# Regrouping a decode backward kernel: four groups of two kv-heads over all batches, and the zero rows as 6 KB packets on one queue

## Chip, cores and metric

One core of a Trainium2 chip. The metric is the device time of one execution in microseconds (us); "span" is the time from the first to the last instruction of the profiled execution, some 1 to 5 us shorter. Engines: PE (TensorE), DVE (VectorE), ACT (ScalarE), POOL (GpSimd), SP (SyncE, used here only to start transfers).

## The reference

A decode step of one token for four batches: attention over the last 1024 of 4096 cached positions (32 query heads, 8 kv-heads of 128), and a GEGLU feed-forward part (512 to 1792), both added to x. What is computed is the output and all gradients.

```python
def _A_ref(x, k_cache, v_cache, wq, wo):
    ...
    W = min(4096, max(256, Sk // 4))                      # 1024 of 4096
    q = (lambda x, *d: x.transpose(*d))((x @ wq).reshape(B, Sq, Hq, Dh), 0, 2, 1, 3)
    k = jnp.repeat(k_cache[:, :, Sk - W:, :], rep, axis=1)
    v = jnp.repeat(v_cache[:, :, Sk - W:, :], rep, axis=1)
    scores = jnp.einsum("bhqd,bhkd->bhqk", q, k) * (Dh ** -0.5)
    p = _softmax(scores, axis=-1)
    o = jnp.einsum("bhqk,bhkd->bhqd", p, v)
    ...
x = A_x
xn = _layernorm(x, axis=-1)
return x + _A_ref(xn, A_k_cache, A_v_cache, A_wq, A_wo) + _B_ref(xn, B_w_gate, B_w_up, B_w_down)
# outputs: that, and jax.vjp of it: dx, dK, dV, dwq, dwo, dw_gate, dw_up, dw_down
```

The gradients of the caches have the caches' size, and three quarters of them are zeros: 50.3 MB of the 81.0 MB that are written.

## The kernel before

Weights first, then the feed-forward part, then one batch after another. Each piece of zeros waits for a point in the scores; each transposed block is copied half by ACT, half by DVE.

```python
        def emit_zero_pieces(step, gate_ap):
            target = (len(zero_pieces) * (step + 1) + nsteps - 1) // nsteps
            while zdone[0] < min(target, len(zero_pieces)):
                nc.gpsimd.affine_select(out=ztile[:], in_=gate_ap, pattern=[[0, ZW]], compare_op=ALU.is_ge,
                                        fill=0.0, base=-1, channel_multiplier=0)
                nc.gpsimd.dma_start(out=zero_pieces[zdone[0]], in_=zsrc)      # 2 MB, rows of 2,048 B
                zdone[0] += 1
        for b in range(B):
            ...
            for g in range(G):
                ...
                    nc.scalar.copy(out=T_sb[:, 0:hw], in_=T_ps_flat[:, 0:hw])
                    nc.vector.tensor_copy(out=T_sb[:, hw:J * P], in_=T_ps_flat[:, hw:J * P])
                ...
            for lhs_src, rmask, og, tg in ((P_b, domr, out_3, "dv"), (dS_b, qmr, out_2, "dk")):
                ...
                        nc.tensor.matmul(mps[:], lhsT=lhs_src[:, j * P:(j + 1) * P], rhs=rhs, start=True,
                                         stop=True)                             # all 128 rows
                ...
                    nc.sync.dma_start(out=dst_full, in_=stg[:].rearrange("p g j d -> p g (j d)"))
    # then: gradients of wo and wq, and wo and wq read once more for the output and dx
```

## Time and profile before

| | before |
|---|---|
| time, median of 3 (range) | 389.94 us (388.05 to 392.74) |
| span, mean granted PE clock | 385.1 us, 0.785 |
| moved by DMA | 120.48 MB, 313 GB/s over the span |

The lines that matter are in the prediction. They show a kernel that changes between stages that are full of transfers and stages in which DMA stands half idle.

### The profile page before, as it was taken

To read this page: it belongs to the slowest core of one execution; us is meant where nothing else is said; L and a number is where in the kernel's file an instruction comes from. 1 tells how busy PE (TensorE), PEld (TensorE's weight loads), DVE (VectorE), ACT (ScalarE), POOL (GpSimd) and SP (SyncE) were. 2 spreads that over 40 slices of the span, in tenths; PEclk is the share of its full clock that TensorE was granted. 3 is DMA by queue.
4 is the path that set the end of the run, shared out by engine and by line. 5 is a ranking of instruction groups with operands and counts; after the bars stand their busy time and mean duration, and the time that the engine had idled before them with its cause. 6 is when DMAs were issued, how large, how long until landed. Compare 5 with 4: busy or idle time off the path is not lost.

```text
span 385.1 us, 6390 instructions
## 1 busy us (share of the span) xinstructions
PE 276.8 (72%) x2524; PEld 143.0 (37%) x2524; DVE 180.3 (47%) x344; ACT 156.2 (41%) x257; POOL 72.7 (19%) x103
## 2 busy tenths in 40 slices
PE   0087897998367949994999489968809768874882
PEld 0075553446133624462546253635206221110340
DVE  3034242545973366636573658355904233331425
ACT  1045253553233535654575437552705332430431
POOL 1000132535565222102202110222222211100000
PEclk9999595896657966997699959995966655555997
DMA  7999999358676649997999699956996999996350
GB/s 269 394 397 418 401 393 366 149 206 323 257 283 265 267 145 397 413 409 283 366 410 410 270 350 376 409 231 265 414 360 247 356 400 403 401 319 218 111 163 1
DMA packets 55181, 120.48 MB, mean 313 GB/s; under 512 B 3360, under 2 KB 21552, under 8 KB 54640
## 3 DMA queue, kind: packets, MB, share of 16 engines
q1 hardware_dynamic: 40400, 64.25, 45.6%
q0 software_dynamic: 14752, 55.84, 36.0%
q8 instruction: 19, 0.31, 0.3%
q14 instruction: 10, 0.08, 0.1%
HBM read 39.07 MB, written 81.01 MB: 312 GB/s over the span
## 4 chain that ended last, share of the span: by engine, by line
PE 32%; DMA 25%; DVE 13%; ACT 13%; issue 9%; SPq 5%; POOL 4%; DVEq 0%; ACTq 0%; POOLq 0%
DMA out_dram<-osb 10%; PE kv_ps L466 9%; ACT T_sb L400 8%; DMA vb<-in_A_v_cache_dram 6%; PE S_ps L404 4%; SPq L159 4%; PE dP_ps L404 3%; DMA wo_sb<-in_A_wo_dram 3%; DMA out_dram<-stg_dk 3%; PE dxa_ps L559 2%; DVE osb L87 2%; DMA wq_c<-in_A_wq_dram 2%; DVE stg_dk L87 2%; POOL out_dram L307 2%; PE od_ps L451 2%
## 5 line engine op out<-in xcount | busy, mean ns | idle before, releaser
L377 POOL TENSOR_SCALAR_AFFINE_SELECT ztile<-vb 128x1024 bf16<-128x1024 bf16 x24 | 25.0, 1043 | 224.5 <-DMA out_dram<-ztile 185.4
L400 ACT COPY T_sb<-T_ps 128x512 bf16<-128x512 bf16 x64 | 37.1, 586 | 38.2 <-PE T_ps L94 35.2
L401 DVE COPY T_sb<-T_ps 128x512 bf16<-128x512 bf16 x64 | 26.9, 422 | 39.0 <-ACT T_sb L400 38.8
L94 PE MATMUL T_ps<-ident,vb 128*128 128x128 bf16 x256 | 28.4, 227 | 0.9 <-DVE T_sb L401 0.9
L404 PE MATMUL dP_ps<-T_sb,dom 128*128 128x512 bf16 x64 | 24.3, 393 | 6.5 <-DVE negm L412 4.0
L94 PE MATMUL T_ps<-ident,kb 128*128 128x128 bf16 x256 | 28.9, 230 | 0.0
L404 PE MATMUL S_ps<-T_sb,qm 128*128 128x512 bf16 x64 | 24.3, 394 | 4.2 <-DVE osb L87 2.3
L466 PE MATMUL kv_ps<-domr,P_b 128*128 128x512 bf16 x64 | 26.9, 533 | 0.5 <-DVE stg_dv L87 0.2
L85 ACT CAST stg_dv<-kv_ps 128x512 bf16<-128x512 f32 x32 | 18.7, 585 | 17.8 <-PE kv_ps L466 17.2
L87 DVE CAST stg_dv<-kv_ps 128x512 bf16<-128x512 f32 x32 | 21.8, 691 | 7.3 <-PE kv_ps L466 6.7
L94 PEld LDWEIGHTS <-kb 128*128 128x128 bf16 x256 | 20.2, 104 | 11.8 <-issue 6.2
L94 PEld LDWEIGHTS <-vb 128*128 128x128 bf16 x256 | 19.8, 102 | 11.8 <-issue 6.0
L94 PE MATMUL woT_ps<-ident,wo_sb 128*128 128x128 bf16 x128 | 12.9, 242 | 14.7 <-DMA wo_sb<-in_A_wo_dram 14.7
L466 PE MATMUL kv_ps<-qmr,dS_b 128*128 128x512 bf16 x64 | 21.4, 376 | 2.5 <-DVE stg_dk L87 0.6
L379 POOL DMA_DIRECT2D out_dram<-ztile x24 | 21.7, 904 | 7.0 <-POOL ztile L377 5.1
L87 DVE CAST stg_dk<-kv_ps 128x512 bf16<-128x512 f32 x32 | 21.7, 692 | 2.2
L85 ACT CAST stg_dk<-kv_ps 128x512 bf16<-128x512 f32 x32 | 18.7, 585 | 4.7 <-PE kv_ps L466 3.6
L529 PE MATMUL dwq_ps<-dq_bp,xn_b 4*128 4x512 bf16 x32 | 15.7, 608 | 5.9 <-ACT osb L85 3.5
L85 ACT CAST osb<-mps 128x512 bf16<-128x512 f32 (+1 forms) x23 | 12.2, 551 | 17.0 <-DMA out_dram<-osb 15.7
L85 ACT COPY woT<-woT_ps 128x512 bf16<-128x512 bf16 x16 | 9.4, 586 | 23.6 <-PE woT_ps L94 18.3
L85 ACT COPY wqT<-wqT_ps 128x512 bf16<-128x512 bf16 x16 | 9.4, 586 | 22.8 <-PE dxa_ps L559 14.5
L87 DVE COPY woT<-woT_ps 128x512 bf16<-128x512 bf16 x16 | 6.8, 424 | 24.4 <-PE woT_ps L94 23.8
(171 smaller groups left out, 461.2 us busy)
## 6 DMA issues: line engine op xcount, KB each, us to landing
out_dram<-ztile POOLq DMA_DIRECT2D x24, 2048.0 KB, 9.4
kb<-in_A_k_cache_dram SPq DMA_DIRECT2D x32, 256.0 KB, 6.3
vb<-in_A_v_cache_dram SPq DMA_DIRECT2D x32, 256.0 KB, 6.3
out_dram<-stg_dv SPq DMA_DIRECT2D x8, 1024.0 KB, 10.6
out_dram<-stg_dk SPq DMA_DIRECT2D x8, 1024.0 KB, 16.6
out_dram<-osb SPq DMA_DIRECT2D x32, 256.0 KB, 5.9
out_dram<-osb POOLq DMA_DIRECT2D x38, 128.0 KB, 5.8
wo_sb<-in_A_wo_dram SPq DMA_DIRECT2D x4, 1024.0 KB, 14.0
```

The costliest lines, as they stand in the source:

```text
L85: nc.scalar.copy(out=out, in_=in_)
L87: nc.vector.tensor_copy(out=out, in_=in_)
L94: nc.tensor.transpose(ps_ap, in_ap, ident[:])
L159: nc.sync.dma_start(out=t[:, i * step:(i + 1) * step, :], in_=src_ap[:, i * step:(i + 1) * step, :])
L307: nc.gpsimd.dma_start(out=og[c * P:(c + 1) * P, f0:f0 + fw], in_=osb[:, 0, 0:fw])
L377: nc.gpsimd.affine_select(out=ztile[:], in_=gate_ap, pattern=[[0, ZW]], compare_op=ALU.is_ge, fill=0.0, base=-1, channel_multiplier=0)
L379: nc.gpsimd.dma_start(out=zero_pieces[zdone[0]], in_=zsrc)
L400: nc.scalar.copy(out=T_sb[:, 0:hw], in_=T_ps_flat[:, 0:hw])
L401: nc.vector.tensor_copy(out=T_sb[:, hw:J * P], in_=T_ps_flat[:, hw:J * P])
L404: nc.tensor.matmul(acc_ps[:, half * 512:(half + 1) * 512], lhsT=lhsT, rhs=T_sb[:, half * 512:(half + 1) * 512], start=(g == 0), stop=(g == ...
L466: nc.tensor.matmul(mps[:], lhsT=lhs_src[:, j * P:(j + 1) * P], rhs=rhs, start=True, stop=True)
L529: nc.tensor.matmul(mps[:, i, :], lhsT=xn_b[:, c * P:(c + 1) * P], rhs=dq_bp[:, jq * 512:(jq + 1) * 512], start=True, stop=True)
```

## The change

Intent: read every weight once, gather all batches of two kv-heads in 128 score rows (four quarters of 32 rows, each a quarter of the positions), do the feed-forward part first, and let the zeros stream ungated on SP's queue as 6,144 B rows while everything else uses POOL's. Cut to its core:

```diff
-    outp = ctx.enter_context(tc.tile_pool(name="outp", bufs=5))
+    outp = ctx.enter_context(tc.tile_pool(name="outp", bufs=3))
-                nc.gpsimd.affine_select(out=ztile[:], in_=gate_ap, ...)
-                nc.gpsimd.dma_start(out=zero_pieces[zdone[0]], in_=zsrc)
+    ZG = 2
+    def zeros():
+        zsrc = bass.AP(tensor=ztile.tensor, offset=ztile.offset, ap=[list(ztile[:].ap[0]), [0, ZG], [1, ZW]])
+        for b in range(B):
+            for g in range(0, G, ZG):
+                for og in (out_2, out_3):
+                    nc.sync.dma_start(out=og[b, g:g + ZG, 0:K0, :].rearrange("g (m j) d -> m g (j d)", m=P),
+                                      in_=zsrc)
-                    nc.scalar.copy(out=T_sb[:, 0:hw], in_=T_ps_flat[:, 0:hw])
-                    nc.vector.tensor_copy(out=T_sb[:, hw:J * P], in_=T_ps_flat[:, hw:J * P])
+                    evac(T_sb[:], T_ps[:].rearrange("p j m -> p (j m)"), 1024, half=True)
-                        nc.tensor.matmul(mps[:], lhsT=lhs_src[:, j * P:(j + 1) * P], rhs=rhs, ...)
+                        nc.tensor.matmul(mps[:].rearrange("p b d -> p (b d)"), lhsT=src[rs, jj * P:(jj + 1) * P],
+                                         rhs=mr[rs, g].rearrange("p b d -> p (b d)"), start=True, stop=True,
+                                         tile_position=(q * RG, 0))             # 32 rows
+        zeros()                  # on SP, straight behind the feed-forward weights
+        load_w(0)                # all other loads and all stores: POOL's queue
+        load_kv(0)
+        load_w(1)
+        ...                      # feed-forward part
+        for t in range(NT):
+            if t + 1 < NT:
+                load_kv(t + 1)
+            softmax(t)
+            odq(t)               # the products with V and K
+            if t + 1 < NT:
+                pre(t + 1)
+            dvdk(t, stage)       # K and V gradients
+            if t + 1 < NT:
+                scores(t + 1)
+            fin(t)               # wo and wq gradients, output, dx
+            if t + 2 < NT:
+                load_w(t + 2)
```

The written order is not the order on the engines: a scheduler places the instructions when the kernel is built.

## The prediction

> **What bounds the kernel now.** I read the page first (engine shares, the 40 slices, the queues), then the table by stages, then the list of waits. No engine is the bound on its own:
>
> ```profile
> span 385.1 us, 6390 instructions
> ...
> PE 276.8 (72%) x2524; PEld 143.0 (37%) x2524; DVE 180.3 (47%) x344; ACT 156.2 (41%) x257; POOL 72.7 (19%) x103
> ...
> DMA  7999999358676649997999699956996999996350
> GB/s 269 394 397 418 401 393 366 149 206 323 257 283 265 267 145 397 413 409 283 366 410 410 270 350 376 409 231 265 414 360 247 356 400 403 401 319 218 111 163 1
> DMA packets 55181, 120.48 MB, mean 313 GB/s; under 512 B 3360, under 2 KB 21552, under 8 KB 54640
> ...
> q1 hardware_dynamic: 40400, 64.25, 45.6%
> q0 software_dynamic: 14752, 55.84, 36.0%
> ...
> HBM read 39.07 MB, written 81.01 MB: 312 GB/s over the span
> ```
>
> The reader is to see that the transfers run at 390 to 418 GB/s in about half of the slices and idle in the others, so the kernel alternates between a DMA-bound and a compute-bound state. The table by stages (length, busy times of PE, PEld, DVE, ACT, POOL, granted clock, DMA share, GB/s) shows which stage is which:
>
> ```profile
> 18.00:38.40 20.40, 14.94 (x259) 12.24 (x260) 7.50 (x17) 9.37 (x16) 0.00 (x0) 1.00 1.05 406
> 38.40:75.50 37.10, 32.22 (x348) 17.52 (x348) 14.34 (x45) 15.24 (x28) 11.06 (x17) 0.72 0.85 324
> 75.50:120.40 44.90, 31.14 (x306) 17.79 (x306) 29.07 (x58) 16.38 (x31) 24.19 (x39) 0.73 0.68 268
> 120.40:142.10 21.70, 15.51 (x129) 8.79 (x130) 10.32 (x20) 9.65 (x16) 5.43 (x7) 0.82 0.55 207
> 142.10:158.20 16.10, 15.37 (x154) 6.73 (x154) 10.67 (x17) 9.38 (x17) 1.93 (x2) 0.71 1.03 403
> ...
> 322.00:346.00 24.00, 18.07 (x39) 3.88 (x37) 9.06 (x8) 8.10 (x8) 1.93 (x2) 0.50 1.01 377
> 346.00:385.00 39.00, 23.06 (x150) 9.59 (x149) 13.73 (x29) 8.78 (x15) 0.00 (x0) 0.81 0.38 123
> ```
>
> Weights come in (18 to 38), the feed-forward part follows (38 to 120, DMA two thirds used), then four batches of some 40 us each (scores and softmax 24, gradients of K and V 16, the latter DMA-bound), then the weight gradients (279 to 346, DMA-bound), then 39 us in which weights are read a second time and DMA moves 123 GB/s. The waits name the reasons:
>
> ```profile
> POOL ztile L377 <- DMA out_dram<-ztile: 185.4, 23, 14.0
> ...
> DVE T_sb L401 <- ACT T_sb L400: 38.8, 53, 2.5
> ACT T_sb L400 <- PE T_ps L94: 35.2, 57, 3.6
> ACT osb L85 <- DMA out_dram<-osb: 35.2, 15, 5.1
> ```
>
> The zeros go one 2 MB piece at a time (POOL waits for the landing of each). In the scores, VectorE waits for ScalarE before it takes its half of the same transposed block: 53 waits, so a block costs 586 + 424 + about 100 = 1.11 us in series, which is the 1.1 us step of ScalarE copies in the chain.
>
> **What the Trainium skill says.** (1) "DMA: Bandwidth & Descriptors", section "Queues, rings and completion order": each DMA engine goes round its queues, one packet at a time. The trace agrees: its DMA records show 4,096 B packets on the software queue and one packet per row (1,024, 2,048, 3,584, 8,192 B) on the hardware queue. In 5 us stretches where both are full the shares follow these sizes: 292 to 125 and 312 to 104 GB/s against 2,048 B rows, 359 to 59 against 1,024 B rows. (2) "PSUM — Partial Sum Buffer", section "PSUM bank collisions raise a hardware error": two engines may not touch one bank and quadrant at once. It fits the 53 waits: the halves of one bank are in series. (3) "TensorE: Matmul & The Clock Gate", Part 3: tiles of 32 rows or columns run together, 2.38 times for three column tiles, 3.07 for four row tiles. No run here shows it yet. (4) "GPSIMD Engine Reference", section "Engine selection": two-input elementwise work takes about twice as long there as on VectorE.
>
> **The change, part by part.**
>
> Traffic. wq and wo are read once: 2 x 4.19 = 8.39 MB less, so 120.48 - 8.39 = 112.1 MB. At the 405 GB/s of the saturated stages the floor is 277 us. The kernel cannot go below some 285 with its start and end, and this floor is 73% of the span of now.
>
> Order of traffic. Zeros (50.3 MB, 32 transfers, no waits) stand on the hardware queue straight behind the feed-forward weights (5.5 MB). Everything else, 56 MB, is on the software queue of POOL. A zero packet becomes 6,144 B against 4,096, so where both queues are full the zeros get 60%, about 243 GB/s, and all loads and gradient stores 162.
>
> Scores of a group. Still 16 blocks of 8 transposes (8 in 0.45 us at full clock, as in the timeline). A block is now copied whole by one engine: ACT about 1.01 us (its 128x1024 casts take 1.01), DVE about 0.68 (4x1024 copies take 0.68), side by side 0.41 per block. PE: 0.45 plus 4 matmuls of 256 columns, 0.15 if column tiles run together, 0.43 if not. So 0.6 to 0.9 us per block in place of 1.11: about 12 us per group, 48 in all against 71.
>
> Softmax of a group. A quarter of the columns (256), but more hops: the maximum and the sums cross the quarters by five small PE operations. About 15 steps of 0.2 to 0.5 us with 0.07 between: 7.3 us, against 7.5 per batch in the chain now. Nothing gained on the path. The products with V and K: 128 small matmuls at 31 ns, 4 us as now.
>
> K and V gradients: 32 casts of 128x512 per group as before, ACT 585, DVE 691 ns, side by side 0.32: 10.5 us, if stores do not hold them. Now 12 to 16.
>
> Before each group: 32 transposes, 4 copies, 64 small matmuls, 5 us. After it (output projection, wo and wq gradients, the part of dx): 6 copies of 1024 (2.5 us side by side) and 16 casts of 512 (5.2 us) lie beside PE's own work, which is longer: 32 matmuls of 512 columns at 215 ns, 48 transposes at 57 ns, 9.6 us at full clock. I take 11 us. The mask products, some 2.4 us each (estimate: 1.21 us on VectorE times two, the skill's factor), lie on POOL beside this.
>
> Sum of a group: 12 + 7.3 + 4 + 10.5 + 5 + 11 = 50 us; with the instructions that the scheduler moves into the softmax gaps (it does so now with gradient matmuls at 142 us) I take 45. Four of them: 180, against four batches of 40 and the 105 after them and the 20 before the feed-forward part now (285).
>
> Start. The first weight is in by 7 us; then POOL's 8.4 MB of loads compete. The second (3,584 B rows, about 46%) lands near 16, the third (1,024 B rows, 17 to 20%, as in the 359 to 59 stretch) near 37, when POOL's loads are through. Feed-forward work: 37 us with 3 store buffers of 0.5 MB, whose 5.5 MB leave at 162 GB/s: done at about 68. Scores, softmax and products of group 0 partly overlap: 92.
>
> Sum. By 92 us the zeros have got 55 x 0.405 - 5.5 - 1.0 = 15.8 MB; 34.5 are left, at 243 GB/s 142 us, until 234. In that time POOL's queue moves 23 MB, and a group needs 12.6 (K and V 4.2, their gradients 4.2, weights 2.1, weight gradients 2.1): 1.83 groups, 78 us each, so DMA sets the pace. From 234 the groups run at their compute time: 3 - 1.83 = 1.17 times 45 = 53, then the last group's gradients, last stores and layer norm, 10.5 + 11 + 5 = 27: 314. The time is 389.94 where the span is 385.1, so I add 5: **319 us**; I shade it to 316, as the overlap may be better than taken.
>
> **Rivals.** (a) DMA stays full to the end: the queues share evenly. Then the zeros last until 262, POOL moves 34.5 MB, 2.7 groups, and the end comes at 262 + 11 + 27 = 300, with 5 more 305; perfectly filled 290. For it: totals of 415 to 418 GB/s are seen where both queues are full. Against it: the shares by packet size above. (b) The zeros win more than 60% or the feed-forward stores hold back group 0 longer: each 10 us of delay before odq(0) or each 4 us more per late group adds about 5 to 10: 325 to 345. For it: in the 292 to 125 and 312 to 104 stretches the bigger packets got more than their sizes' two to one. (c) PE becomes the bound: if tiles run in series, the K and V gradients take 128 x 215 ns = 27.5 us of PE in place of 9, and the scores 64 x (0.43 - 0.15) = 18 us more, together 36 us over the four groups; and the clock falls to half in stages full of evictions (0.50 at 322 to 346). Groups of 58 us would give about 335. Against it: PE is dense in the scores, where the clock is 0.93 to 1.0. (d) The gradients' waits only move: stores of POOL's queue stand behind loads that wait for buffers; that is part of (b).
>
> **Range and chances.** Floor 290, main sum 316, rivals (b) and (c) 335 to 345. Range 292 to 342. All of these lie more than 2% below 389.94 (382), so faster 0.97, same 0.02, slower 0.01.
>
> **What would show it right or wrong.** Right: HBM read 30.7 MB and written 81.0; zeros' queue at about 240 GB/s and DMA share near 1.0 until 210 to 240 us, then a fall to some 230 GB/s with PE, ACT and DVE denser; waits of copies on stores in the feed-forward part; no waits of DVE on ACT in the blocks' copies; scores of about 12 us per group. Wrong: DMA full to the end (a); groups after the zeros over 55 us (c); the third feed-forward weight much before or after 37; POOL waiting for something other than buffers.

## The result, and the profile after

**343.89 us** (median of 4, 342.86 to 344.13), beside 389.0 for the kernel before in the same rounds. The ratio is 0.886 (95% 0.881 to 0.892). Ratios here are the mean time of one kernel's fast runs over that of the other's of the same rounds, so not quite the ratio of the quoted medians. Executions over 1.5% slower than the fastest of the same kernel are left out of the means. Faster as expected, but above the predicted range of 292 to 342.

The page of the kernel after, to be laid beside the page lines in the prediction:

```profile
span 342.4 us, 6207 instructions
...
PE 245.6 (72%) x2630; PEld 136.6 (40%) x2630; DVE 158.8 (46%) x308; ACT 130.7 (38%) x202; POOL 81.2 (24%) x116
...
PEclk9999999955555995559955556569855559955585
DMA  6999999999999999999999998995369781062736
GB/s 247 381 377 377 396 420 424 421 423 419 414 404 401 409 412 370 417 422 418 381 418 393 413 390 289 375 390 150 133 237 346 290 305 46 0 247 96 274 137 232
...
q0 software_dynamic: 14592, 55.84, 43.2%
q1 hardware_dynamic: 11600, 55.86, 41.0%
...
HBM read 30.68 MB, written 81.01 MB: 326 GB/s over the span
```

The bytes and the picture are as predicted: transfers are full until the zeros are out, then fall. The zeros' last piece is issued at 172 us and their records end near 213. From there PE is busy nine tenths of the time, and its clock is mostly 0.5. The chain that ended last, its DMA pieces (start, length, what; all in us):

```profile
2.52 36.66 DMA wd_sb<-in_B_w_down_dram
...
68.78 13.44 DMA out_dram<-osb_d x2
82.22 20.96 DMA out_dram<-osb_g x3
...
170.92 29.58 DMA out_dram<-osb_o
```

The third feed-forward weight lands at 39.2. Between 69 and 103 the path is the landing of feed-forward gradient stores (`osb_d`, `osb_g`), and from 171 to 201 it is one landing of a wo gradient, 29.6 us. The table by stages (stretch, length, busy times of PE, PEld, DVE, ACT, POOL, granted clock, DMA share, GB/s) shows these two, then a stretch with K and V gradients, then a whole late group:

```profile
68.80:103.30 34.50, 20.32 (x64) 6.53 (x64) 12.15 (x21) 11.24 (x21) 6.78 (x11) 0.50 1.02 415
...
171.00:200.60 29.60, 4.03 (x12) 2.03 (x11) 3.03 (x9) 1.74 (x5) 2.84 (x4) 0.50 1.02 410
209.80:226.20 16.40, 16.40 (x111) 4.69 (x109) 10.88 (x21) 9.41 (x18) 10.15 (x11) 0.50 0.94 351
...
257.50:311.30 53.80, 50.58 (x549) 28.11 (x546) 31.72 (x59) 27.78 (x44) 13.47 (x16) 0.66 0.52 192
```

In the second line the compute engines nearly stand and DMA moves 410 GB/s. In the third PE is busy for all of 16.4 us, at half clock; 9.9 us of it are K and V gradients, the rest the output projection and the preparation of the next group, which the scheduler placed between them. The waits (engine, line, what for: us in total, times, longest) name the standstill, and show that DVE no longer waits for ACT in the transposed blocks:

```profile
ACT osb_q L88 <- DMA out_dram<-osb_o: 26.8, 2, 25.3
...
DVE osb_q L89 <- DMA out_dram<-osb_o: 25.1, 2, 24.8
...
DVE T_sb L89 <- PE T_ps L248: 18.4, 28, 1.4
```

The copies of the wq gradient (`osb_q`) need one of the three buffers, and these are free only when earlier stores (`osb_o`) have landed.

### The profile page after: what moved, and what is told of

Same layout as the page of the kernel before. It is cut to its first block, busy times and chain, and to the rows that moved or that the text cites. A ratio compares the mean times of both kernels' runs of the same rounds, so it can differ in the third digit from the quotient of the medians.

```text
span 342.4 us, 6207 instructions
## 1 busy us (share of the span) xinstructions
PE 245.6 (72%) x2630; PEld 136.6 (40%) x2630; DVE 158.8 (46%) x308; ACT 130.7 (38%) x202; POOL 81.2 (24%) x116
## 4 chain that ended last, share of the span: by engine, by line
PE 59%; DMA 30%; ACT 4%; DVE 4%; issue 2%; SPq 0%; ACTq 0%; DVEq 0%
PE kv_ps L334 11%; PE T_ps L248 11%; DMA wd_sb<-in_B_w_down_dram 11%; DMA out_dram<-osb_o 10%; DMA out_dram<-osb_g 6%; PE ao_ps L348 5%; PE od_ps L313 4%; DMA out_dram<-osb_d 4%; PE woT_ps L203 3%; PE wqT_ps L365 3%; PE dxa_ps L370 2%; PE dxf_ps L488 2%; PE dP_ps L256 2%; PE tq_ps L354 2%; PE dwq_ps L388 2%
## 5 line engine op out<-in xcount | busy, mean ns | idle before, releaser
L88 ACT COPY T_sb<-T_ps 128x1024 bf16<-128x1024 bf16 x26 | 26.1, 1012 | 25.5 <-PE T_ps L248 25.5
L89 DVE COPY T_sb<-T_ps 128x1024 bf16<-128x1024 bf16 x38 | 25.8, 690 | 18.8 <-PE T_ps L248 18.4
L89 DVE CAST stg_dv<-kv_ps 128x512 bf16<-128x512 f32 x30 | 20.2, 688 | 10.6 <-PE kv_ps L334 10.1
L88 ACT CAST stg_dk<-kv_ps 128x512 bf16<-128x512 f32 x34 | 19.5, 586 | 10.8 <-PE kv_ps L334 10.5
L203 PEld LDWEIGHTS <-wo_sb 128*128 128x128 bf16 x128 | 11.6, 131 | 27.6 <-issue 26.5
L89 DVE CAST osb_q<-dwq_ps 128x512 bf16<-128x512 f32 x16 | 10.6, 686 | 25.9 <-DMA out_dram<-osb_o 25.1
L334 PE MATMUL kv_ps<-domr,P_b 32*128 32x512 bf16 x64 | 20.9, 576 | 1.2 <-DVE stg_dv L89 0.6
L334 PE MATMUL kv_ps<-qsmr,dS_b 32*128 32x512 bf16 x64 | 20.8, 601 | 0.0
L88 ACT CAST osb_q<-dwq_ps 128x512 bf16<-128x512 f32 x16 | 8.8, 585 | 28.5 <-DMA out_dram<-osb_o 26.8
L248 PE MATMUL T_ps<-ident,vb 128*128 128x128 bf16 x256 | 19.4, 237 | 0.0
L348 PE MATMUL ao_ps<-wo_sb,oT 128*4 128x512 bf16 x32 | 18.5, 590 | 0.0
L89 DVE CAST osb_g<-dwg_ps 128x512 bf16<-128x512 f32 (+1 forms) x16 | 8.7, 586 | 15.7 <-DMA out_dram<-osb_g 9.3
L176 POOL DMA_DIRECT2D vb<-in_A_v_cache_dram x16 | 11.5, 720 | 18.6 <-PE od_ps L313 14.7
L391 POOL DMA_DIRECT2D out_dram<-osb_q x8 | 5.7, 711 | 40.1 <-DVE rr L286 27.1
## 6 DMA issues: line engine op xcount, KB each, us to landing
wo_sb<-in_A_wo_dram POOLq DMA_DIRECT2D x4, 1024.0 KB, 12.8
```

The costliest lines, as they stand in the source:

```text
L88: return nc.scalar.copy(out=out, in_=in_)
L89: return nc.vector.tensor_copy(out=out, in_=in_)
L176: nc.gpsimd.dma_start(out=tl[:].rearrange("p g j d -> p g (j d)"), in_=src[b, t * GP:(t + 1) * GP, K0:Sk, :].rearrange("g (m j) d -> m g ( ...
L203: nc.tensor.transpose(wT_ps[:, i, c, :], wo_sb[:, 2 * h2 + i, c * P:(c + 1) * P], ident[:])
L248: nc.tensor.transpose(T_ps[:, j, :], blk[:, g, j, :], ident[:])
L334: nc.tensor.matmul(mps[:].rearrange("p b d -> p (b d)"), lhsT=src[rs, jj * P:(jj + 1) * P], rhs=mr[rs, g].rearrange("p b d -> p (b d)"), s ...
```

## The experiments

Theory A: the zeros' stream holds up POOL's queue more than was counted, through the three store buffers. Theory B: what holds it is the total rate of the DMA engines, so a hold-up removed in one place comes back in another. Theory C: the compute itself is longer than counted, since matmuls with few rows (4 or 32) leave the clock at 0.50. "Odq ends" are the ends of the products with V and K, one per group; I use them as milestones.

### e1: no zeros

```diff
-        zeros()
+        pass
```

> The changed kernel without its 32 zero transfers (two outputs wrong on purpose); the order on every engine is the same. Theory A (the zero stream holds back the loads and stores of the software queue): the wait of the feed-forward stores, 34.5 us in the changed kernel, falls to about 16, the standstill of 30 us at 171 us is gone, the step from the first group's products to the second's falls from 78 to about 48 us, the end comes at about 293 us span, 296 us time. Theory B (the zeros are hidden, PE at its half clock sets the pace of the groups): at most 10 us less than 344. The third feed-forward weight stays at about 39 us under both, as only the loads of POOL compete with it there.

302.13 us (outputs 2 and 3 wrong; the compute engines' order unchanged). Two of its four runs are slow; the fast ones, 298.75 and 300.83, average 299.8. The zeros cost 44 us. But compute alone takes 297 us of span, where the terms of the prediction without zeros add up to 68 + 24 + 3 x 45 + 27 = 254. By stages, from the table by stages of e1 (the feed-forward gradients, then the steps between odq ends):

```profile
65.80:89.10 23.30, 20.85 (x77) 7.00 (x76) 15.00 (x25) 13.80 (x25) 6.74 (x11) 0.59 0.52 197
117.20:167.70 50.50, 48.01 (x544) 27.72 (x540) 29.80 (x56) 26.19 (x41) 15.39 (x18) 0.70 0.71 245
167.70:214.10 46.40, 43.05 (x508) 23.02 (x505) 29.00 (x55) 23.58 (x38) 17.39 (x21) 0.72 0.72 255
214.10:266.60 52.50, 49.23 (x550) 27.40 (x547) 31.59 (x59) 27.77 (x44) 13.51 (x16) 0.70 0.53 197
```

PE is busy 93 to 95% of each group step, at a clock of 0.70 to 0.72. So C has a part, and so has A or B: of the 45.5 us between the two spans, 14.9 come before odq(0) (132.1 against 117.2), 27.1 in the first step (77.6 against 50.5), and 3.5 after.

One thing in POOL's queue is not equal, though the expectation says that the order on every engine is: among the first group's four gradient stores, two stand elsewhere than in the changed kernel, where the weight load of a later group goes ahead of them. e2 and e5 have e1's order of these stores. The difference can hardly have cost much, since that queue is full in the changed kernel from 136 to 202 us (162 GB/s, beside 247 for the zeros), but it keeps e1 and e2 from being one-change experiments.

### e2: zeros in rows of 2,048 B

```diff
-        zsrc = bass.AP(..., ap=[list(ztile[:].ap[0]), [0, ZG], [1, ZW]])          # 32 transfers of 1.5 MB
+        zsrc = bass.AP(..., ap=[list(ztile[:].ap[0]), [0, G], [1, J * Dh]])       # 24 transfers of 2 MB
```

> Same queue, same place, same bytes of zeros, but in rows of 2,048 B (24 transfers of 2 MB, the layout of the kernel before) in place of 6,144 B. Theory A with shares by packet size: where both queues are full the zeros get 1 part against 2 (some 135 to 270 GB/s) in place of 250 to 165; the zeros last until some 250 us, the store wait of the feed-forward part falls to 22 to 25 us and the step from the first to the second group's products to 55 to 60; time 308 to 320 us. If the queues share by bytes or by turns of another size, or if the zeros cost only through the bandwidth they use: within 5 us of 344.

322.13 us, ratio 0.834 (0.829 to 0.838), correct: 22 us less, with every compute instruction in the same place. The pieces are also larger, and POOL's order is e1's, so the clean proof that the row length costs time is e15 against e16 below. The gain lies in the first group step (58.3 in place of 77.6). The shorter wait in the feed-forward part, 22 to 25 us, that was expected did not come: its copies end at 100.7 in place of 104.4.

### e3: five store buffers

```diff
-    outp = ctx.enter_context(tc.tile_pool(name="outp", bufs=3))
+    outp = ctx.enter_context(tc.tile_pool(name="outp", bufs=5))
```

> Five in place of three store buffers for the feed-forward and weight gradients. Theory A1 (the copies stand still because three buffers wait for stores that queue behind others at 165 GB/s): feed-forward store phase 34 to about 27 us, and the standstill of 25 us before the copies of the wq gradient is gone at least in part; 320 to 332 us. Theory A2 (only bandwidth counts, the backlog is the same however many buffers): 338 to 345 us.

342.49 us, ratio 0.879 (0.868 to 0.889); fast runs, 337.88 and 341.51, are 4 us below the changed kernel on average, and the intervals overlap. The profile ends the feed-forward part at 92.7 in place of 103.3 and odq(0) at 121.9 in place of 132.1; then PE stands 25.5 us for a later group's wq load, which landed at 208 (197 in the changed kernel):

```profile
PE q_ps L213 <- DMA wq_sb<-in_A_wq_dram: 25.5, 1, 25.5
```

I read this as theory B at first. It is weaker than that: the scheduler had also put other transfers ahead on POOL's queue (two K and V loads before this one), which e11 shows can cost as much.

### e4: first loads ahead of the zeros

```diff
+        load_w(0, nc.sync)
+        load_kv(0, nc.sync)
+        load_w(1, nc.sync)
         zeros()
-        load_w(0)
-        load_kv(0)
-        load_w(1)
```

> The first loads of wo, wq, K and V (8.4 MB) go to the hardware queue behind the feed-forward weights and ahead of the zeros. Theory A: the third feed-forward weight lands at about 18 us in place of 39, the feed-forward part starts 20 us sooner, and as the time until the zeros end is worth 50/78 of its length in groups, the end comes some 13 us sooner: 328 to 333 us. If the start is hidden behind the zeros anyway: 340 to 345 us.

337.84 us, ratio 0.874 (0.867 to 0.880). The third feed-forward weight is 17 us sooner (its transposes start at 22.6 against 39.2), odq(0) ends 17 us sooner (114.7), and only 6 us are left at the end, where 11 to 16 were expected. Most of the rest was probably lost to order, as e15 suggests below: the scheduler had moved transfers on POOL's queue here too.

### e5: e4 and e2 together

> The two parts that helped, together: first loads ahead of the zeros on the hardware queue, zeros in rows of 2,048 B. If the loss at the start and the share of the zeros are separate costs, the gains add (22 us and 6 us of the pair of runs before, or more, as the start is no longer paid back by waits): 306 to 316 us. If they are one cost seen twice: 320 to 324.

311.32 us, ratio 0.796 (0.790 to 0.803), correct. The gains of the two alone, 22 and 6, make 28; together they give 32.6. Its compute instructions stand in the changed kernel's order again, as e2's do.

### e6, e7: few rows and the clock

Both without zeros, against e1. e6 multiplies all 128 rows in the K and V gradients (values wrong). e7 fills the operands of 4 rows (dy, xn and the four gradients) with zero rows up to 128, which changes no value.

```diff
# e6
-                        nc.tensor.matmul(..., lhsT=src[rs, jj * P:(jj + 1) * P], rhs=mr[rs, g]..., tile_position=(q * RG, 0))
+                        nc.tensor.matmul(..., lhsT=src[:, jj * P:(jj + 1) * P], rhs=mr[:, g]...)
# e7, one of six such edits
-    dy_b = const.tile([B, D], BF16, name="dy_b")
+    dy_b = const.tile([P, D], BF16, name="dy_b"); nc.gpsimd.memset(dy_b[:], 0.0)
```

> The kernel without zeros (302 us) with the K and V gradient matmuls over all 128 rows in place of one tile of 32 rows each (wrong values on purpose; the order on every engine is the same). Theory C (matmuls over 32 rows leave the granted clock at 0.50): the clock in these stretches rises to 0.75 or more, each stretch is 3 to 5 us shorter, 285 to 292 us. Theory D (the clock stays, the tiles of 32 rows ran side by side and now run in series, a pair in 0.86 us in place of 0.53): each group 5 us longer, about 320 us. Neither matters, the copies out of PSUM set the pace: 300 to 304.

> The kernel without zeros with the operands of 4 rows of the weight-gradient matmuls padded by zero rows to 128 (those values stay right). Theory C (few rows in use keep the clock at half): the feed-forward gradients, 23 us at a clock of 0.50, take 14 to 17, the wo and wq gradients 1 us less per group: 288 to 293 us. If the clock follows something else, as the time that PE waits: 300 to 304, one or two for the clearing of the pads included.

e6 took 290.48 us and e7 286.03, against 299.8 for e1's fast runs. Mean clocks: 0.762 in e1, 0.832 in e6, 0.806 in e7. What moved, one matmul of each kind (minimum, median and maximum in ns, first and last start, shapes). In e1:

```profile
L334 PE MATMUL kv_ps<-qsmr,dS_b x64: 577/602/605, 125.6 to 278.2; 32*128 32x512 bf16 x64
...
L520 PE MATMUL dwg_ps<-dhg_bp,xn_b x16: 412/602/629, 72.7 to 80.7; 4*128 4x512 bf16 x12, 4*128 4x256 bf16 x4
```

The first of them in e6, with 128 rows:

```profile
L334 PE MATMUL kv_ps<-qsmr,dS_b x64: 379/379/390, 128.1 to 271.5; 128*128 128x512 bf16 x64
```

The second in e7, with 128 rows:

```profile
L521 PE MATMUL dwg_ps<-f_bp,xn_b x32: 269/376/390, 62.5 to 75.8; 128*128 128x512 bf16 x24, 128*128 128x256 bf16 x8
```

Each record shown is a third shorter with four or thirty-two times the rows, as the clock rises: over the four stretches of K and V gradients it is 0.50 to 0.56 in e1 and 0.75 to 0.89 in e6. Theory C stands in kind. In size, full rows in the K and V gradients are worth 8 to 9 us (8 of span, 9.3 of fast time), and not through these matmuls themselves. Those of V, which run first, keep a median of 587 ns in e6, and all 128 hold PE for 40.6 us in e1 and, with 125 recorded, for 44.5 in e6. Matmuls of 32 rows often run side by side: in e1 52 of them start within 100 ns of the one before, in e6 none. In the changed kernel one holds PE for 0.53 us before the next starts, and a pair, started together, also for 0.53:

```profile
218.00 0.60 PE L334 MATMUL kv_ps<-qsmr,dS_b 32*128 32x512 bf16 x1
218.53 0.59 PE L348 MATMUL ao_ps<-wo_sb,oT 128*4 128x512 bf16 x1
219.05 0.61 PE L334 MATMUL kv_ps<-qsmr,dS_b 32*128 32x512 bf16 x2
```

What got shorter is the work around them: the output projection (`ao_ps`) from 18.5 to 12.4 us of PE, the transposes of the scores (`T_ps`) from 41.4 to 36.8. e7's gain of 13 to 14 us is confounded: the fills on POOL delayed its loads, so the third weight landed 9 us sooner (30.3 against 39.4). Its feed-forward gradients took 19.2 us against 23.3, at a clock of 1.00; the groups kept their length. These two, 9.1 and 4.1 us, account for its 12.8 us of span.

### e8 and e11: rows of 1,024 and 3,072 B, and an order that nobody asked for

```diff
# both on e5
-            for y in range(K0 // 1024):      # rows of 2,048 B, 24 transfers
+            for y in range(K0 // 512):       # e8: 1,024 B, 48 transfers of 1 MB
+            for y in range(K0 // 1536):      # e11: 3,072 B, 16 transfers of 3 MB
```

> As the run before, with zeros in rows of 1,024 B (48 transfers of 1 MB). By packet size the zeros get one part against four where both queues are full, but 1,024 B packets move at 22.3 GB/s per DMA engine against 24.4 for 2,048 B (46 and 84 ns in the records of the kernel before). If the share is what counts: 300 to 310 us. If the lower rate takes it back, as the whole 112 MB need about 300 us then: 310 to 322.

> e5_loads_2k with zero rows of 3,072 B in place of 2,048 (16 transfers of 3 MB). One packet a turn says shares of 3,072 to 4,096, that is 43% to the zeros where both are full of stores, against 33% for 2,048 and 60% for 6,144; e8 showed that the law fails for 1,024 B rows. If the law holds between 2,048 and 6,144: zeros' share 0.43, and a time between e5's 311.3 and e4's 337.8, about 316 to 322. If the split has an even floor (about half each below 4,096 B), share 0.5 and within 3 us of e5.

345.8 and 338.97 us: both far slower than e5, and both misses. The waits of e11:

```profile
DVE stg_dv L89 <- DMA out_dram<-stg_dk: 24.7, 2, 22.8
...
ACT stg_dv L88 <- DMA out_dram<-stg_dk: 23.3, 2, 21.7
```

e5 has no wait of that kind. The timeline of POOL's queue (start, length, engine, line, transfer, idle before) tells why. First the first group's gradient stores in e5:

```profile
120.90 0.80 POOL L338 DMA_DIRECT2D out_dram<-stg_dv  x1
...
130.11 0.75 POOL L338 DMA_DIRECT2D out_dram<-stg_dk  x1 [2.73 <-issue]
```

Then in e11, the load that stands ahead of them, the first of them and the last:

```profile
183.71 0.72 POOL L176 DMA_DIRECT2D vb<-in_A_v_cache_dram  x1
184.42 1.63 POOL L338 DMA_DIRECT2D out_dram<-stg_dk  x2
...
189.90 0.75 POOL L338 DMA_DIRECT2D out_dram<-stg_dv  x1 [1.55 <-DMA kb<-in_A_k_cache_dram]
```

They are issued some 60 us later, behind later groups' wo, wq, K and V loads, which wait for their buffers. The four staging buffers stay full, and the next copies stand. The scheduler had changed the order with the size of the zeros' transfers (e8 and e11 are equal to each other in it), so row length and order were mixed up in these two. e4's order differs too.

### e13, e14: an edit that was not applied

> The changed kernel with zero rows of 3,072 B (16 transfers of 3 MB), loads where they were; its PE, VectorE and ScalarE instructions stand in exactly the order of the changed kernel and of e2_zero_2k_rows, unlike e4, e8 and e11. In 2 us bins of e8 and e11 where the other queue is really full, the zeros sent 1.0 to 1.1 packets per packet of the other queue at every row length, so the slow e11 (339.0) should come from its order of stores and loads on POOL's queue (stores of K gradients behind loads that wait for buffers), not from the rows. If so: zeros' share 43% and a time between e2 (322.1) and the changed kernel (343.9), 327 to 335 us. If rows of 3,072 B are in themselves as bad as 6,144: 341 to 345 us.

> The same with zero rows of 1,024 B (48 transfers of 1 MB), same order of instructions as the changed kernel. If one packet a turn holds and e8's 345.8 came from its order: zeros' share 20% where both are full, but their packets move at a lower total rate (about 360 in e8 against 390 with 2,048 B), so the zeros last to the end and the time is near e2's: 316 to 328 us. If rows of 1,024 B are slow in themselves (rate, or several packets to a turn): 338 us or more.

323.89 and 323.38 us. The row length had another name in the source, the replacement found nothing, and both kernels were e2 again. They say nothing of what they were for; with e2's 322.13 they show how well a kernel repeats.

### e15, e16, e17: the row length alone

One kv-head per transfer leaves every engine and POOL's queue in e5's order at any row length (compared instruction by instruction).

```diff
# R_ = 3072, 1536 or 512 positions: rows of 6,144, 3,072 or 1,024 B
+                    nc.sync.dma_start(out=og[b, g:g + 1, y * R_:(y + 1) * R_, :].rearrange("g (m j) d -> m g (j d)", m=P), in_=zsrc)
```

> A correction first: e13 and e14 did not carry their edit (the row length in the source they came from was written with another name, and nothing was replaced): both were e2 again, 2,048 B rows, and count as repeats of it (322.1, 323.9, 323.4 us). This run is e5_loads_2k (311.3 us) with zero rows of 6,144 B, one kv-head per transfer (64 transfers), which leaves every engine's instructions, POOL's transfers too, in e5's order. One packet a turn gives the zeros 60% where both queues are full, as in e4 (337.8 us), whose order differs: 330 to 341 us. If e4 was slow for its order: under 325 us.

> The same with zero rows of 3,072 B (128 transfers), again in e5's order on every engine. If one packet a turn holds and e11 (339.0 us, the same rows) was slow because its order puts the K and V gradients' stores behind loads: share 43%, a time between e5 and the 6,144 B run, 315 to 326 us. If rows of 3,072 B are as bad as 6,144 B in themselves: 336 to 341 us.

> The same with zero rows of 1,024 B (384 transfers), in e5's order. If one packet a turn holds and e8 (345.8 us) was slow for its order: the zeros get 20% where both are full, POOL's queue waits less than in e5, but the packets' total rate is lower (about 360): 305 to 318 us. If rows of 1,024 B are slow in themselves: 338 us or more.

The table is worked out from the DMA records, in 2 us bins; rates are medians. "Full" are bins in which the zeros' packets numbered 0.85 to 1.15 for each 4,096 B packet of POOL's queue (41 of 61 bins after, 54 of 88 in e5, 65 of 97 in e16, 25 of 94 in e17; counts shift by a few with the bins' start). That the other bins are those in which POOL's queue had too little to send is not shown. Bins picked by this ratio can't prove that the queues take turns, so here are also whole stretches in which both send all the time: 241 and 167 GB/s in e15 (120 to 160 us), 174 and 240 in e16 (116 to 136), 143 and 268 in e5 (118 to 140), that is 0.96, 0.97 and 1.07 packets of the zeros for one of POOL's. e17 has no such stretch (1.42 over 112 to 130 us).

| zero rows | kernel | us (ratio to before) | odq ends | full bins: zeros, POOL GB/s | zeros alone, GB/s |
|---|---|---|---|---|---|
| 6,144 B | e15 | 328.17 (0.851) | 112.7, 187.3, 237.7, 295.4 | 246, 166 | 416 |
| 3,072 B | e16 | 310.04 (0.805) | 110.1, 167.2, 217.8, 277.0 | 172, 236 | 400 |
| 2,048 B | e5 | 311.32 (0.796) | 111.2, 168.2, 218.7, 278.4 | 141, 266 | 388 |
| 1,024 B | e17 | 350.6 (0.909) | 104.9, 158.9, 208.5, 261.2 | 73, 307 | 266 (e8: 353) |

All three times lie outside what turns by packet let expect (330 to 341, 315 to 326 and 305 to 318 us). Four things follow. **One packet each in turn** fits at 6,144, 3,072 and 2,048 B; at 1,024 B it is not shown. **The row length costs time**: e15 and e16 ran on one chip in the same rounds, with every engine and queue in the same order, and differ by 18 us (328.17 and 310.04; the pieces, 768 and 384 KB, follow from the rows). **The order costs some 25 to 29 us**: e11 and e16 have the same rows and differ by 338.97 against 310.04 (25 us by their ratios, on two chips; their pieces, 3 MB and 384 KB, differ too, so it is the stores' late issue and the waits above that name the order). e4 against e15, both with 6,144 B, is 10 us (their pieces also differ, 1.5 MB and 768 KB). So loads first are worth 15.7 us with the compute engines' order unchanged (343.89 to 328.17, 14 us by the ratios), where e4 had shown 6. e5 and e16 are a per cent apart, one ahead in ratio, the other in time: I call them equal. **Smaller rows end badly for another reason**: e17's groups run as if there were no zeros (its steps are 54.0, 49.6 and 52.7 us, e1's 50.5, 46.4 and 52.5), its PE is done at 285 us, and then 60 us of zeros are left. Pieces of 128 KB get only 266 GB/s alone, where e8's of 1 MB with the same rows get 353. SP's own waits of e17:

```profile
SPq L190 <- DMA out_dram<-ztile: 54.5, 47, 3.0
```

The rate in the 40 slices of e17's page, where the last six are the zeros alone:

```profile
GB/s 253 385 361 386 372 248 318 350 357 272 238 247 361 408 353 283 288 397 329 398 395 335 258 390 365 406 410 257 287 314 281 360 336 321 267 259 268 266 265 207
```

Whether 1,024 B rows in 1 MB pieces and in e5's order would do better than e5 was not run.

### e9, e10, e12, e18: towards a better kernel

e9 is e5 with e7's fills; e10 adds five store buffers; e12 is e9 with e6's full rows (wrong values); e18 is e10 with 3,072 B rows, in e10's order.

> e5_loads_2k (311.3 us) with the operands of the weight-gradient matmuls padded with zero rows to 128, as in e7, but here the loads at the start are not on POOL's queue, so the pads' memsets can't move the third feed-forward weight (check: it must land within 2 us of e5's time; wdT within 2 us). Theory C (matmuls of 4 rows leave the granted clock at 0.50): clock of the feed-forward gradient stage 0.8 to 1.0, that stage about 4 us shorter if stores let it, groups unchanged within 1 us each as in e7: 305 to 309 us. If e7's 16 us were mostly the earlier landing (9 us) the gain here is at most 7. Rival, that all of e7's gain was clock: 295 to 298. Results stay correct.

> e9 with five store buffers in place of three. With the zeros as 2 KB rows POOL's stores get about half of the rate, so the wait in the buffers is shorter than in e3, and e4's early loads mean that nothing stands behind the stores at the start. If buffers still bound the feed-forward part: FFN end 5 to 10 us sooner, and 3 to 6 us of the whole. If the total bandwidth does (as e3 showed: the standstill only moved), within 2 us of e9.

> e9 with the K and V gradient matmuls over all 128 rows as in e6 (wrong values of outputs 2 and 3, on purpose). Without zeros this alone was worth 8 to 11.6 us. Compute bound with zeros at 2 KB rows: 8 to 12 us off e9. If DMA is the bound until some 270 us, as e5's rate of 361 GB/s says (floor 112 MB at 405 GB/s is 277), most of it is hidden: 0 to 5 us off.

> The last run, a candidate for the best version: e10_pads_outp5 (300.1 us) with zero rows of 3,072 B, one kv-head per transfer (128 transfers); every engine and POOL's queue stay in e10's order. In e10 the DMA engines are full to the end (mean 375 GB/s, zeros until the last 10 us), and 2,048 B packets alone move at 364 to 380 GB/s where 3,072 B packets alone moved at 397. If total bandwidth bounds e10: 293 to 298 us. If POOL's share does (43% to the zeros in place of 33%): 301 to 308 us.

Measured: e9 307.96 us, e10 300.08 (ratio 0.769, 0.764 to 0.775), e12 300.57, e18 296.50 (ratio 0.770, 0.765 to 0.776). e9 bears e7 out: with the loads no longer moved, the fills are worth 3 us (307.96 against 311.32, on two chips; the intervals of the ratios overlap). The stretch of the feed-forward gradients in the tables by stages shows why. In e5:

```profile
49.10:81.90 32.80, 20.82 (x75) 7.08 (x75) 14.65 (x25) 13.26 (x25) 6.81 (x11) 0.57 1.03 393
```

In e9:

```profile
49.20:82.00 32.80, 18.92 (x76) 6.82 (x75) 14.73 (x25) 13.15 (x25) 6.82 (x11) 0.73 1.03 392
```

In e10:

```profile
49.20:70.30 21.10, 15.95 (x74) 5.85 (x75) 14.12 (x24) 12.50 (x23) 6.27 (x10) 0.84 1.04 402
```

The fills raise the clock from 0.57 to 0.73 and the stretch stays at 32.8 us, as the three buffers' stores bound it. With five buffers it takes 21.1. So buffers, which seemed to give nothing in e3, give 8 us here. e12 says that full rows would be worth 7 us more even with the zeros, if values could be kept. In e10 DMA is full to the end, as the page's slices show:

```profile
DMA  6999999999999999999999999999999999999992
```

e18 is 3.6 us below e10 by medians, but they ran on different chips, and their ratios to the kernel before are equal. Both beat the kernels before and after: e10 by 23% and 13%.

## Why the prediction was wrong

The direction and the mechanism were right; three terms of the sum were mis-sized, two of them the same way.

| term, us of span | predicted | after | without zeros (e1) |
|---|---|---|---|
| third feed-forward weight lands | 37 | 39.2 | 39.4 |
| feed-forward part ends | 68 | 103.3 | 89.1 |
| odq(0) ends | 92 | 132.1 | 117.2 |
| first group step | 78 | 77.6 | 50.5 |
| the other two steps | 117 | 101.6 | 98.9 |
| last odq to the end | 27 | 31.1 | 30.3 |
| sum | 314 | 342.4 | 296.9 |

The predicted 117 is the rest of the three steps: 314 - 27 - 92 - 78. What failed:

1. **"Feed-forward work: 37 us with 3 store buffers ... done at about 68."** It took 64 us from the weight's landing in place of 31. Without zeros it takes 50: so 19 of the excess are its own work, 14 the stores behind the zeros. The overlap is what failed: the prediction let the 34 us in which 5.5 MB leave at 162 GB/s run beside the rest of the work. But the first store copy starts at 66.7 us, after 27 us of transposes and matmuls, and the copies end only at 104.4. The work is a series (transposes, vector chain, transposes, gradients), the last of it at a clock of 0.59 without zeros. This one term, 33 us, is more than the whole miss of 28. e3 and e10 confirm the buffers' part (10.6 and 12 us sooner, e3 against the changed kernel, e10 against e9), e7 the clock's part (4 us).
2. **"So 0.6 to 0.9 us per block", "Nothing gained on the path", "I take 45"** for a group. The group alone is 46.4 to 52.5 (mean 49.8), so the first sum, 50, was right, and the 5 us taken off for overlap were not there. The scores took 12.9 to 14.0 us in place of 12. The K and V gradient matmuls held PE for 10.3 us a group, near the 10.5 of their copies, but lay in stretches of 15.7 to 23.4 us, shared with other work at half clock. Of rival (c), the half clock came, and e6 shows that rows have a part in it; the tiles in series did not, as the pair above shows.
3. **"34.5 are left ... until 234."** The zeros were out near 213, since POOL's queue was often not full before 132 (120 GB/s over the feed-forward stores, 68.8 to 103.3 us, where 162 was taken) and left them the rate. So about two groups ran after them where 1.17 were counted, and that gave back 15 us.

What held: the shares of 60 to 40 (252 to 164 GB/s measured, 243 to 162 predicted), the contended step of 78, the bytes, the wait of copies on stores, no wait of DVE on ACT, the fall of DMA after the zeros. The mask products took 1.88 us where 2.4 was estimated. Of the rivals, (b) with its 325 to 345 was the nearest: the feed-forward stores did hold back group 0. It was treated as a tail, though its premise (three buffers of 0.5 MB behind a stream that takes 60%) stood in the diff. Rival (a) is refuted: DMA falls at the end. The range stopped at 342 though the rivals ran to 345, and the 5 us added from span to time were 1.7 in the profiled run; the latter hid 3 us of the miss in span.

What stays open: whether e3's missing gain was lost to total rate or to its changed order. e10 against e9 shows that buffers help once the zeros take less, though there too the scheduler moved two stores and some compute instructions. Open too is whether 1,024 B rows take turns like the others.

## What to carry to other kernels

A stream without waits on its own queue is not free: it takes from the other queue in the ratio of the packet sizes, so set the row length with both rates in mind (here 2 to 3 KB) and put what is needed first in front of it. When an edit changes the sizes of transfers, compare the order of the instructions on every engine and queue before reading the time: here an unasked order cost 25 to 29 us and hid the effect under test. And count a series of small stages by measured stages, not by the sum of their busiest instructions.

## What the Trainium skill lacked or had wrong

- "DMA: Bandwidth & Descriptors", section "Queues, rings and completion order": taking turns by packet fits at three lengths (241:167, 174:240 and 143:268 GB/s of 6,144, 3,072 and 2,048 B against 4,096 B), if one record of the trace is taken for a packet; the page's packet is of several descriptors, and these rates can't tell how many records make a turn. The page has no trn2 rates for a stream alone at these row lengths (416, 400 and 388 GB/s here, and 266 where pieces of 1,024 B rows are 128 KB).
- "TensorE: Matmul & The Clock Gate", section "Part 4: PE-mode transpose": it says that full clock does not engage for transposes. In the kernel before, it was granted at 1.00 from 25.2 to 38.9 us, in which PE ran transposes and matmuls of 4 columns in turn; in the kernel after, transposes mixed with wider matmuls ran at 1.00 from 44.0 to 65.8. No run has transposes alone, and the traces don't show whether these ran in the page's transpose mode. (Clock records begin only at these starts, 25.2 and 44.0, and the tables count the time before as 1.00: in the kernel after, the first 16 transposes took 118 ns each, those from 49.6 us on 63.) The page does not tie the clock to the number of rows: here it stood at 0.50 with PE busy for 16.40 of 16.40 us, 9.9 of them in matmuls of 32 rows, and full rows raised it (from 0.50 to 0.56 in the stretches of e1 to 0.75 to 0.89 in those of e6).
- No page that I read has it: a changed transfer size can change the built order of everything else (e11 against e16, 25 to 29 us).
